# A fused transformer block on one core: two-head chunks in place of four-head ones in the attention products, paired 64-row remainders in the first dense layer, DMA transposes, and a shared PSUM bank

## The chip, the cores and the metric

The kernel runs on one core of a Trainium2 chip. The metric is the device time of one execution in microseconds (us), as the median of several runs. The profile is one further execution, in which the hardware profiler records each instruction. Its span, from first to last instruction, is some 2 us shorter than the device time.

Engines: PE is TensorE (matrix products), PEld is its weight load, DVE is VectorE, ACT is ScalarE, POOL is GpSimd, SP issues most DMA transfers. PSUM is the memory that PE's products are summed in; here it is used as eight banks.

## The reference, cut to what matters

S = 2048 tokens, D = 448, H = 16 heads of 28 features, F = 1792.

```python
xn  = layernorm(x)                                   # no scale, no bias
q, k, v = split(xn @ wqkv)                           # 16 heads of 28
phi_q = concat(softmax(q@w_phi), softmax(-q@w_phi))  # 56 features a head
phi_k = concat(softmax(k@w_phi), softmax(-k@w_phi))
kv  = phi_k^T @ v ;  z = sum over tokens of phi_k    # one 56 x 28 matrix a head
o   = (phi_q @ kv) / (phi_q @ z + 1e-6)
out = x + o @ wo + silu(xn @ w1) @ w2
```

This is linear attention: kv needs all tokens, so no token's output can start before the last token's key is done. The two dense layers (dense 1 is `xn @ w1`, dense 2 is `silu(..) @ w2`) depend on nothing of attention, and can fill gaps. `w_phi` is multiplied into the q and k weights on the chip at the start (the "fold").

## The kernel before: the parts that matter

The program is built from operations with reads, writes, a priority and a guessed duration. A list scheduler on the host orders them once. On the chip every engine then works through its own fixed list, and waits on semaphores where an operand comes from another engine. Priority 0 is the most urgent.

```python
# dense 1: contraction 448 = 4 x 112 rows; one silu per block
for kt in range(4):
    e.matmul(hps, w1_sb[:, kt, ft*128:(ft+1)*128], xnT_sb[:, kt, tok0:tok0+ntok], ...)   # 112 rows
act(hT[:, ft, ...], hps, Silu)

# keys: token-major, all + signs (s=0), then all - signs (s=1); chunks of four heads
for s in range(2):
    for g in range(4):
        e.matmul(bank[3+s][0:112, g*116:(g+1)*116], Ek[:, sl, s, g*112:(g+1)*112],   # 112 columns of weights
                 vaug[:, sl, 4*g:4*g+4, :])                                          # 4 x 29 = 116 columns

# queries: feature-major (EqT), not normalised; U has 4 heads x 30 = 120 columns
for s in range(2):
    for g in range(4):
        e.matmul(bank[3+s][:, g*120:(g+1)*120], EqT[:, cs, g, s, tokens], KVZ[:, s, g])
# DVE: R2, Dd, den, rden, Gq, then o12 (896 elements in f32); POOL: o_sum = o12[+] + o12[-]
# PE: 4 transposes of o_sum; ACT: copy; PE: wo

# dense 2 of a tile: own bank, ACT copies it to Y_sb, POOL adds x; after wo, DVE adds Y_sb
```

Here `vaug` is v with a column of ones for each head, so that one product gives kv and z. A block of four heads against four heads makes a 112 x 116 product of which only the four blocks on the diagonal are wanted; a mask removes the others.

The softmax here doesn't subtract the row's maximum and nothing guards it: scores larger than these inputs give would overflow.

## Time and profile before

187.69 us median (187.44 to 188.22, 4 runs). From the page of the profile: first busy time and share per engine, then the granted TensorE clock in 40 slices of the span (in tenths), then the chain of work that ended last.

```profile
span 185.7 us, 3256 instructions
...
PE 176.4 (95%) x1272; PEld 105.1 (57%) x1272; DVE 96.0 (52%) x215; ACT 99.9 (54%) x197; POOL 75.6 (41%) x94
...
PEclk9999999999999999999999999999999999999997
...
PE 77%; DVE 7%; DMA 6%; SPq 4%; POOL 2%; issue 1%; ACT 1%; POOLq 0%; DVEq 0%; ACTq 0%
...
```

PE is busy for 95% and makes up 77% of the chain. The clock is at full speed up to the last slice (0.7), which lies after the last product. But the busy time of PE is not its work: the products overlap, and the mean of one in the groups (352 ns for 448 columns) is a latency. The work is what one product adds to a stream of them. The chain of waits, which merges neighbours, shows it; its columns are start, duration and what.

```profile
...
58.73 12.09 PE psum L552 x56
...
108.61 1.51 PE psum L640 x8
...
```

56 products of 512 columns in 12.09 us are 216 ns each, 8 of 448 in 1.51 us are 189 ns each. The groups of instructions by line and shape give the counts: after the bar, busy us and the mean ns of one.

```profile
...
L682 POOL TENSOR_TENSOR scr<-scr 128x448 bf16<-128x448 f32 x16 | 18.1, 1134 | 33.7 <-DVE scr L676 25.3 <-PE psum L696 8.4
...
L676 DVE TENSOR_TENSOR scr<-psum,Gq 128x896 f32<-128x896 f32 x16 | 17.4, 1090 | 0.7
...
L660 PE MATMUL psum<-KVZ,EqT 112*128 112x120 bf16 x128 | 10.4, 216 | 0.0
...
L604 PE MATMUL psum<-vaug,Ek 128*112 128x116 bf16 x128 | 9.3, 214 | 0.0
...
L669 DVE SCALAR_TENSOR_TENSOR den<-Dd 128x16 f32<-128x16 f32 x16 | 6.2, 391 | 0.5
...
```

Here the reader sees the 128 key products of 116 columns (L604), the 128 query products of 120 columns (L660), the o product on DVE (1090 ns) and the addition on POOL (1134 ns). In the middle of attention, these form the chain of waits, from the query product (L660) to the transposes (L688):

```profile
...
142.75 0.43 PE psum L660 x8
...
143.82 0.37 DVE den L669
...
144.81 1.10 DVE scr L676
...
145.98 1.14 POOL scr L682
...
147.17 0.43 PE psum L688 x4
...
```

Counts times spacing, over all products but the warm-up ones, is **164.5 us of PE work**. The span splits as follows (worked out from the start of every product in the trace):

| | before, us |
|---|---|
| PE work | 164.5 |
| PE time lost up to 18.5 us, where dense 1 first runs without gaps | 10.6 |
| PE time lost from there to the last product | 7.6 |
| after the last product | 3.0 |
| span | 185.7 |

### The profile page before, as it was taken

How to read it: one execution, taken by the hardware profiler on the slowest of the kernel's cores; microseconds unless marked ns; L12 is line 12 of the kernel's file. 1: busy time of each engine (PE TensorE's matmuls, PEld its weight loads, DVE VectorE, ACT ScalarE, POOL GpSimd, SP SyncE). 2: the span in 40 equal slices, each digit the busy share in tenths (PEclk: the TensorE clock that was granted, in tenths of full speed). 3: DMA queues.
4: the chain of work that ended last, by engine and by line, in shares of the span. 5: the costliest groups of instructions: out<-in, count | busy, mean ns of one | idle time of the engine just before them, and what ended most of it. 6: DMA issues, size and time to landing. Idle time of an engine off the chain costs nothing.

```text
span 185.7 us, 3256 instructions
## 1 busy us (share of the span) xinstructions
PE 176.4 (95%) x1272; PEld 105.1 (57%) x1272; DVE 96.0 (52%) x215; ACT 99.9 (54%) x197; POOL 75.6 (41%) x94
## 2 busy tenths in 40 slices
PE   6978999999998999999999999999999999999982
PEld 6766866654444445556666666555555555555540
DVE  2439893050003000166777742478987888646762
ACT  2575496736663675838767765535444553513221
POOL 4136175000000000289888983165255235443651
PEclk9999999999999999999999999999999999999997
DMA  4999990000000000000000000001001000000011
GB/s 136 235 281 220 252 306 17 2 4 0 0 0 0 0 4 0 0 0 4 2 0 0 4 0 0 0 4 48 28 25 47 32 25 28 25 25 25 6 47 49
DMA packets 11375, 8.72 MB, mean 47 GB/s; under 512 B 992, under 2 KB 11360, under 8 KB 11360
## 3 DMA queue, kind: packets, MB, share of 16 engines
q1 hardware_dynamic: 11360, 8.51, 18.3%
q8 instruction: 10, 0.16, 0.4%
q14 instruction: 5, 0.04, 0.1%
HBM read 6.68 MB, written 1.84 MB: 46 GB/s over the span
## 4 chain that ended last, share of the span: by engine, by line
PE 77%; DVE 7%; DMA 6%; SPq 4%; POOL 2%; issue 1%; ACT 1%; POOLq 0%; DVEq 0%; ACTq 0%
PE psum L552 22%; PE psum L640 20%; PE psum L577 7%; PE psum L582 7%; DMA scr<-in_A_wqkv_dram 6%; PE psum L627 5%; PE psum L696 5%; SPq L445 4%; PE psum L604 4%; PE psum L660 3%; POOL scr L682 2%; DVE scr L676 2%; PE psum L688 2%; DVE den L669 1%; PE psum L513 1%
## 5 line engine op out<-in xcount | busy, mean ns | idle before, releaser
L552 PE MATMUL psum<-xnT_sb,w_sb 112*128 112x512 bf16 (+1 forms) x280 | 51.9, 337 | 0.8 <-ACT hT L555 0.5
L640 PE MATMUL psum<-w_sb,hT 128*128 128x448 bf16 x224 | 50.2, 352 | 0.8 <-DVE xnT_sb L541 0.6
L555 ACT ACTIVATE hT<-psum 128x256 bf16<-128x256 f32 (+1 forms) x70 | 34.4, 511 | 21.5 <-PE psum L552 21.0
L552 PEld LDWEIGHTS psum<-xnT_sb,w_sb 112*128 112x128 bf16 x280 | 26.4, 98 | 21.8 <-ACT hT L555 1.1
L645 POOL TENSOR_TENSOR Y_sb<-Y_sb,x_sb 128x448 f32<-128x448 f32 x16 | 16.5, 1033 | 52.9 <-ACT Y_sb L643 49.8
L592 DVE TENSOR_REDUCE Sk<-Ek 128x32 f32<-128x896 bf16 x16 | 17.3, 1084 | 28.4 <-ACT Ek L586 28.4
L682 POOL TENSOR_TENSOR scr<-scr 128x448 bf16<-128x448 f32 x16 | 18.1, 1134 | 33.7 <-DVE scr L676 25.3
L640 PEld LDWEIGHTS psum<-w_sb,hT 128*128 128x128 bf16 x224 | 21.0, 97 | 18.6 <-DVE xnT_sb L541 0.8
L596 POOL TENSOR_TENSOR Ek<-Ek,Rk 128x896 bf16<-128x896 bf16 x16 | 27.1, 1699 | 2.9 <-DVE Rk L594 1.7
L631 ACT ACTIVATE EqT<-psum 112x512 bf16<-112x512 f32 x32 | 17.6, 597 | 10.3 <-PE psum L627 10.3
L586 ACT ACTIVATE Ek<-psum 128x448 bf16<-128x448 f32 x32 | 15.6, 544 | 9.1 <-PE psum L577 5.0
L690 ACT ACTIVATE scr<-psum 112x512 bf16<-112x512 bf16 x16 | 9.5, 596 | 18.7 <-PE psum L688 18.7
L627 PE MATMUL psum<-xnT_sb,Wfull 112*112 112x512 bf16 x64 | 19.4, 379 | 0.0
L676 DVE TENSOR_TENSOR scr<-psum,Gq 128x896 f32<-128x896 f32 x16 | 17.4, 1090 | 0.7
L541 DVE COPY xnT_sb<-psum 112x512 bf16<-112x512 bf16 x12 | 4.8, 417 | 24.3 <-PE psum L535 24.3
L577 PE MATMUL psum<-Wfull,xnT_sb 112*128 112x448 bf16 x64 | 16.5, 352 | 0.0
L696 PE MATMUL psum<-wo_sb,scr 112*128 112x448 bf16 x64 | 14.8, 352 | 1.6 <-ACT scr L690 1.6
L643 ACT ACTIVATE Y_sb<-psum 128x448 f32<-128x448 f32 x16 | 8.8, 550 | 12.4 <-PE psum L640 5.8
L582 PE MATMUL psum<-Wfull,xnT_sb 112*128 112x448 bf16 x64 | 14.9, 352 | 0.0
L699 DVE TENSOR_TENSOR scr<-psum,Y_sb 128x448 bf16<-128x448 f32 x16 | 9.9, 620 | 6.9 <-POOL Y_sb L645 2.3
L521 DVE BATCH_NORM_STATS2 st<-x_sb 128x6 f32<-128x448 bf16 x16 | 9.6, 605 | 6.9 <-DMA x_sb<-in_A_x_dram 6.9
L665 DVE RECIPROCAL R<-psum 128x32 f32<-128x32 f32 x16 | 5.7, 357 | 11.7 <-PE psum L660 11.7
(48 smaller groups left out, 179.1 us busy)
## 6 DMA issues: line engine op xcount, KB each, us to landing
out_dram<-scr SPq DMA_DIRECT2D x16, 112.0 KB, 1.7
w_sb<-in_B_w_dram SPq DMA_DIRECT2D x7, 224.0 KB, 5.7
w_sb<-in_B_w_dram SPq DMA_DIRECT2D x1, 1568.0 KB, 14.9
x_sb<-in_A_x_dram SPq DMA_DIRECT2D x3, 448.0 KB, 8.1
scr<-in_A_wqkv_dram SPq DMA_DIRECT2D x1, 784.0 KB, 10.3
Wfull<-in_A_wqkv_dram SPq DMA_DIRECT2D x1, 392.0 KB, 10.3
wo_sb<-in_A_wo_dram SPq DMA_DIRECT2D x1, 392.0 KB, 11.0
x_sb<-in_A_x_dram SPq DMA_DIRECT2D x2, 112.0 KB, 2.4
```

The source lines that it names most:

```text
L552: P.op("pe", d_mm(ntok), lambda e, lhsT=lhsT, rhs=rhs, hps=hps, kt=kt: e.matmul(hps, lhsT, rhs, start=(kt == 0), stop=(kt == KT - 1)), rea ...
L555: P.op("act", d_act(ntok), lambda e, dsth=dsth, hps=hps: e.activation(dsth, hps, ACTF.Silu), reads=[hps], writes=[dsth], table="silu", nam ...
L577: P.op("pe", d_mm(D), lambda e, lhsT=lhsT, rhs=rhs, pkb=pkb, kt=kt: e.matmul(pkb, lhsT, rhs, start=(kt == 0), stop=(kt == KT - 1)), reads= ...
L582: P.op("pe", d_mm(D), lambda e, lhsT=lhsT, rhs=rhs, vb=vb, kt=kt: e.matmul(vb, lhsT, rhs, start=(kt == 0), stop=(kt == KT - 1)), reads=[lh ...
L592: P.op("dve", d_dve(896), lambda e, E3=E3, sl=sl: e.tensor_reduce(Sk[:, sl, :], E3, AXL.X, ALU.add), reads=[E3], writes=[Sk[:, sl, :]], na ...
L596: P.op("pool", d_pool(896, 1.77), lambda e, E3=E3, sl=sl: e.tensor_tensor(E3, E3, Rk[:, sl, :, None].broadcast_to([128, 32, DH]), ALU.mult ...
L627: P.op("pe", d_mm(512), lambda e, lhsT=lhsT, rhs=rhs, pqb=pqb, kt=kt: e.matmul(pqb, lhsT, rhs, start=(kt == 0), stop=(kt == KT - 1)), read ...
L631: P.op("act", d_act(512), lambda e, dstE=dstE, pqb=pqb, s=s: e.activation(dstE, pqb, ACTF.Exp, scale=(1.0 if s == 0 else -1.0)), reads=[pq ...
L640: P.op("pe", d_mm(D), lambda e, lhsT=lhsT, rhs=rhs, ft=ft: e.matmul(fb, lhsT, rhs, start=(ft == 0), stop=(ft == FT - 1)), reads=[lhsT, rhs ...
L676: P.op("dve", d_dve(896), lambda e: e.tensor_tensor(dsto, U4[:, :, :, 0:DH], Gq[:, q, :].rearrange("p (s h) -> p s h", s=2)[:, :, :, None] ...
L682: P.op("pool", d_pool(448, 2.26), lambda e: e.tensor_tensor(o_sum[:, q, :], o_both[:, q, 0, :], o_both[:, q, 1, :], ALU.add), reads=[o_bot ...
L696: P.op("pe", d_mm(D), lambda e, lhsT=lhsT, rhs=rhs, g=g: e.matmul(ob, lhsT, rhs, start=(g == 0), stop=(g == G - 1)), reads=[lhsT, rhs], wr ...
```

## The change

The intent is less PE work, and a shorter path through DVE and POOL in attention.

- Dense 1 contracts 3 x 128 rows and a remainder of 64. Two blocks' remainders lie in rows 0 to 63 and rows 64 to 127 of the array, and are issued one after the other, so that they may run side by side. They are batched, two or three pairs (4 or 6 products) at a time, and one pair alone once: 11 batches.
- q is computed token-major like k, normalised by POOL, and transposed by DMA (16 transposes). Half of the tiles of xn are transposed by DMA too.
- The 56 features of a head now lie together, (+28, -28), so a 112-wide chunk is two heads, and the key and query products stream 2 x 29 = 58 columns. As many products as before, half as wide.
- With normalised q, attention needs den, rden and o on DVE, and nothing on POOL.
- Half of the dense-2 tiles accumulate into the bank of wo: no eviction, no addition between. The other eight ("y tiles") are kept apart in f32, at the lowest priority, as filler for PE.
- Dense 1 begins with blocks of 512 tokens in place of 256, and one silu takes two banks (28 of 1024 columns in place of 70 smaller ones).

```diff
+ w1_sb = phT[:, 0:3, 0:FF] ; w1r_sb = phT[:, 3, 0:HF]     # rows 0-63: blocks 0-6; rows 64-127: blocks 7-13
+ def rem(st):
+     return [(banks[b0 + i], w1r_sb[64*i:64*i+64, fp*128:(fp+1)*128],
+              xnT_sb[64*i:64*i+64, 3, tok], st, not st) for i in range(2)]
+ def ffn1_group(blocks):                                   # 2 or 3 pairs
+     ops3[0][0](True)                                      # 2 x 3 full products of the first pair
+     pe_mms(rems, "ffn1_rem", ...)                         # the remainders of all pairs
+     ... fulls of the other pairs ...
...
- for kt in range(KT):  # pq_mm, 112 features x 512 tokens
+ for i in (1, 0):      # k, q: 128 tokens x 448 features, exp into E_sb as (head, sign, feature)
...
+ def kv(t):
+     for c in range(CC):                                   # 8 chunks of two heads
+         mm(banks[5][0:KP, c*2*DA:(c+1)*2*DA], E_sb[:, sl, 1, c*KP:(c+1)*KP],
+            vaug[:, t % NV, 2*c:2*c+2, :], ...)            # 58 columns, weights 112 wide
+ def phi_q(t):
+     P.op("pool", ..., phq = Eq * Rq)
+     P.dma(lambda e: e.dma_start_transpose(out=phT[:, :, t*128:(t+1)*128], in_=phq...))
...
+ den = U3[:, :, DH] + EPS_DEN ; rden = 1/den ; o = U3[:, :, 0:DH] * rden     # all on DVE
...
+ P.cur_prio = 3
+ for t in range(NYT):                # NYT = 8
+     y_tile(t, [6, 7][t % 2])        # dense 2 in a bank of its own, DVE adds x into Y_sb
+ for i, t in enumerate(order_t):     # 8, 0, 9, 1, ...
+     b = OUT_BANKS[ob_cnt[0] % 4]    # OUT_BANKS = [6, 7, 4, 5]
+     q = att(t)                      # priority 0
+     if t < NYT: finish_tile(t, q, b, Y_sb[:, t, :], True)
+     else:
+         P.cur_prio = 2 ; ffn2(t, b, False)
+         P.cur_prio = 0 ; finish_tile(t, q, b, x_sb[:, t, :], False)   # wo into the same bank
```

## The prediction

> **What bounds it now.** TensorE. The page gives PE 95% busy, the chain of waits 77% PE, and the granted clock is 0.995. Busy time counts overlapped latency, so I count start-to-start spacing from the timeline instead: 216 ns for 512 columns (56 matmuls in 12.09 us), 189 ns for 448 (14 in 2.65), 109 ns for 256, about 52 ns for the 116- and 120-column products and for transposes 56 ns. Summed over the instruction counts of the groups view (without the 64 warm-up products) this is 164.5 us of needed PE work: dense 1 48.5, dense 2 42.4, k and v 24.2, q 13.8, wo 12.1, kv and attention products 13.3, transposes and weight fold 10.2. The rest of the 185.7 us span: about 9.5 us lost before 18.5 us (weights arriving, 256-token blocks), about 2 in 18.5 to 110 us, 2 in 110 to 163, 3 in 163 to 183, and 2.8 after the last matmul.
>
> **What the change does to PE work (estimates from those spacings).**
> - Dense 1: contraction 448 = 3x128 + 64 instead of 4x112; two 64-row remainders run side by side in the array. 168x216 + 28 pairs x 216 = 42.3 us, plus about 0.2 us per switch group, 11 groups: 44.6 against 48.5. Saves 4. (The Trainium skill, "TensorEngine Tiling", Key Properties: tiles work in parallel; changing the mode drains the array. No run here shows either yet.)
> - q token-major: 64x189 instead of 64x216: saves 1.7.
> - kv and attention products in two-head chunks: 58 columns instead of 116 and 120, same count. If streaming alone counted, about 27 ns each and 6.5 us saved; the 112-column weight load of the kv product may hold it near 50. I take 3.3.
> - 8 of 16 xn tiles transposed by DMA: 32 PE transposes less, 1.8.
> Sum: 154 us, so about 10.3 saved.
>
> **Other engines.** The DVE/POOL chain in attention (2.5 us, then a POOL add of 1134 ns) becomes den, rden, o, about 1.1 us, without a POOL step; Y evictions on ACT and POOL adds vanish. That removes most of the loss after 110 us. In the qkv phase the costs per tile are PE 2.7 us, ACT 2.7 (4x544 + 550), DVE 2.5 to 3, POOL 3.4 (two 1699 ns multiplies). POOL is slowest there, 54 us in all, but eight dense-2 tiles (21 us of PE) fill that phase to 64 us, so PE should still bind.
>
> **Start.** Wqk now comes before w1, so dense 1 starts near 10 us instead of 8; but fold and transposes run meanwhile and 512-token blocks follow. I expect 7 to 8 us lost against 9.5. Middle and end: about 6.5 us lost, and 2.8 after.
>
> **Prediction.** 154 + 7.5 + 6.5 + 2.8 = 171 us span, 1.9 more as timed: **173.0 us**, range **168.0 to 179.0**. Chances: faster by over 2% 0.93, within 2% 0.05, slower 0.02.
>
> **What would show it right.** PE still near 95% busy and first in the chain; dense-1 PE time down by about 4 us with rem pairs starting together; 58-column spacing under 52 ns; attention without DVE/POOL waits in the chain.
>
> **What would make it wrong.** Remainder pairs that don't overlap (+6 us); 58-column products held at 50 ns by weight loads (+3); POOL or ACT becoming the pace of the qkv phase (up to +8); DMA transposes taking several us each or waiting behind loads, starving attention; a start waiting for w1 past 12 us.

## The result, and the profile after

172.17 us median (171.73 to 172.53, 4 runs) against 187.69. The ratio is 0.9165, 95% interval 0.9139 to 0.919. A ratio here is the mean time of one kernel's fast runs over that of the other's in the same rounds, so it is not quite the ratio of the medians. Executions over 1.5% slower than the fastest of the same kernel are left out of the means. The same parts of the page:

```profile
span 170.6 us, 2962 instructions
...
PE 160.1 (94%) x1170; PEld 88.6 (52%) x1176; DVE 92.0 (54%) x179; ACT 85.3 (50%) x135; POOL 68.9 (40%) x82
...
PE   6779986999999999999999999999999996999993
...
PEclk9999999999999999999999999999999999999999
...
PE 81%; DVE 6%; DMA 5%; SPq 3%; POOL 2%; issue 1%; ACT 0%; DVEq 0%
...
```

PE is as busy as before, in a shorter span. Besides the start and the end, one slice is not full: the 6 near 142 us. The groups that answer to those of before:

```profile
...
L671 DVE TENSOR_TENSOR o_sb<-psum,rden 128x448 bf16<-128x448 f32 x16 | 9.7, 619 | 0.7 <-PE psum L433 0.3
...
L421 PE MATMUL psum<-vaug,E_sb 128*112 128x58 bf16 x128 | 8.8, 210 | 0.0
L421 PE MATMUL psum<-xnT_sb,phT 64*128 64x512 bf16 x56 | 8.0, 380 | 0.0
L421 PE MATMUL psum<-KVm,phT 112*128 112x58 bf16 x128 | 6.3, 190 | 0.0
...
L666 DVE TENSOR_SCALAR den<-psum 128x16 f32<-128x16 f32 x16 | 2.6, 166 | 1.8 <-PE psum L421 1.6
...
```

Both 58-column products occur 128 times, as before. Their latencies differ (210 and 190 ns), and so do their spacings: 8 key products take 28 ns for the first and 52 for each of the others (0.39 us in all), 8 query products take 0.23 us, 29 ns each. The o product is 619 ns, not 1090, and den is 166, not 391. (Six records of full dense-1 products are missing, 162 for 168. They are counted as work.) The account of the span:

| | before | after | difference | predicted difference |
|---|---|---|---|---|
| PE work | 164.5 | 153.9 | -10.6 | -10.3 |
| lost at the start (to 18.5; to 27.7 us) | 10.6 | 12.0 | +1.4 | -2.0 (9.5 to 7.5) |
| lost from there to the last product | 7.6 | 1.6 | -6.0 | -0.5 (7 to 6.5) |
| after the last product | 3.0 | 3.1 | 0 | 0 |
| span | 185.7 | 170.6 | -15.1 | -14.7 (185.7 to 171) |

(The predicted column does not add up to its last row: the prediction's account of the kernel before was 1.9 us short of the span, above all at the start, where it has 9.5 for 10.6.) The start is cut at different times, where dense 1 first runs on. At one cut, 27.7 us, the loss is 11.6 before and 12.0 after, and the rest 6.6 and 1.6. At 18.5 us, the cut of the prediction, the changed kernel has lost 9.3. And of the 5.5 us lost after 110 us before, 1.9 are left (such sums of spacings are good to some 0.3 us). So the total was right, and PE work was right, but the lost time lay elsewhere than was said. Where does PE lose time now? In the timeline of PE at the start (columns: start, duration, engine, line, operation, count, and idle time before it with the releaser):

```profile
...
12.38 3.18 PE L421 MATMUL psum<-xnT_sb,phT 128*128 128x512 bf16 x15 [0.82 <-DVE xnT_sb L440]
...
24.42 0.40 PE L433 MATMUL psum<-ident,xn_sb 128*128 128x128 bf16 x4 [0.40 <-DVE xnT_sb L440]
...
25.86 0.40 PE L433 MATMUL psum<-ident,xn_sb 128*128 128x128 bf16 x4 [0.34 <-DVE xnT_sb L440]
26.78 0.40 PE L433 MATMUL psum<-ident,xn_sb 128*128 128x128 bf16 x4 [0.52 <-DVE xnT_sb L440]
27.69 1.47 PE L421 MATMUL psum<-xnT_sb,phT 128*128 128x512 bf16 x6 [0.52 <-DVE xnT_sb L440]
...
```

Dense 1 starts at 12.38. At 24 us dense 1 of the first 512 tokens is done. Of the next four tiles' transposes, those of one tile have been fitted in before; three tiles are left, one after the other through one PSUM bank, each waiting for DVE to empty it, with some products of the fold between. Dense 1 goes on at 27.69. And in attention:

```profile
...
143.14 0.93 PE L421 MATMUL psum<-wo_sb,oT_sb 112*128 112x448 bf16 x4 [0.72 <-DVE Y_sb L651]
144.76 1.50 PE L421 MATMUL psum<-wo_sb,oT_sb 112*128 112x448 bf16 x7 [0.69 <-ACT oT_sb L436]
```

PE idles for 1.4 us (0.72 + 0.69), first for DVE writing `Y_sb`: the last y tile. The second wait is for ACT's copy of the transposed o.

### The profile page after: what moved, and what is told of

The parts are those of the page before. It is cut to its first block, busy times and chain, and to the rows that moved or that the text cites. A ratio compares the mean times of both kernels' runs of the same rounds, so it can differ in the third digit from the quotient of the medians.

```text
span 170.6 us, 2962 instructions
## 1 busy us (share of the span) xinstructions
PE 160.1 (94%) x1170; PEld 88.6 (52%) x1176; DVE 92.0 (54%) x179; ACT 85.3 (50%) x135; POOL 68.9 (40%) x82
## 4 chain that ended last, share of the span: by engine, by line
PE 81%; DVE 6%; DMA 5%; SPq 3%; POOL 2%; issue 1%; ACT 0%; DVEq 0%
PE psum L421 79%; DMA x_sb<-in_A_x_dram 5%; SPq L477 3%; PE psum L433 2%; DVE st L529 2%; POOL rstd L533 2%; DVE xn_sb L536 1%; DVE xnT_sb L440 1%; DVE mv L530 1%; DVE xn_sb L538 1%; POOL ve L531 1%; DVE Y_sb L651 0%; DVE out_sb L684 0%; ACT oT_sb L436 0%; DVEq L793 0%
## 5 line engine op out<-in xcount | busy, mean ns | idle before, releaser
L603 DVE TENSOR_REDUCE Ssum<-E_sb 128x64 f32<-128x1792 bf16 x16 | 31.8, 1985 | 42.8 <-ACT E_sb L436 42.8
L421 PE MATMUL psum<-xnT_sb,phT 128*128 128x512 bf16 (+1 forms) x218 | 44.8, 380 | 2.0 <-DVE xnT_sb L440 1.3
L611 POOL TENSOR_TENSOR E_sb<-E_sb,Rrec 128x896 bf16<-128x896 bf16 x16 | 27.1, 1699 | 41.3 <-DVE Rrec L605 41.3
L436 ACT ACTIVATE hT<-psum 128x1024 bf16<-128x1024 f32 x28 | 28.7, 1024 | 18.1 <-PE psum L421 18.1
L436 ACT ACTIVATE E_sb<-psum 128x448 bf16<-128x448 f32 (+1 forms) x68 | 33.5, 594 | 5.2 <-PE psum L433 3.9
L421 PEld LDWEIGHTS psum<-xnT_sb,phT 128*128 128x128 bf16 (+1 forms) x224 | 17.2, 97 | 27.3 <-issue 6.2
L421 PE MATMUL psum<-Wfull,xnT_sb 128*128 128x448 bf16 x128 | 29.1, 352 | 0.0
L627 POOL TENSOR_TENSOR phq<-E_sb,Rrec 128x896 bf16<-128x896 bf16 x16 | 27.0, 1700 | 0.0
L421 PEld LDWEIGHTS psum<-Wfull,xnT_sb 128*128 128x128 bf16 x128 | 12.3, 99 | 10.6
L421 PE MATMUL psum<-wo_sb,oT_sb 112*128 112x448 bf16 x64 | 14.4, 352 | 1.4 <-DVE Y_sb L651 0.7
L421 PE MATMUL psum<-wv_sb,xnT_sb 128*128 128x448 bf16 x64 | 15.2, 352 | 0.0
L436 ACT ACTIVATE vaug<-psum 128x448 bf16<-128x448 f32 x16 | 9.0, 562 | 11.6 <-PE psum L421 11.5
```

Source lines behind the costliest of these rows:

```text
L421: r = e.matmul(dst, lhsT, rhs, start=st, stop=sp, skip_group_check=True)
L436: P.op("act", d_act(n), lambda e: e.activation(dst, src, func, scale=scale), reads=[src], writes=[dst], table=table, name=name, **keys)
L603: P.op("dve", 1950, lambda e: e.tensor_reduce(Ssum[:, sl, :], E64, AXL.X, ALU.add), reads=[E64], writes=[Ssum[:, sl, :]], name="Ssum")
L611: P.op("pool", 1700, lambda e: e.tensor_tensor(E3, E3, Rrec[:, sl, 32:64, None].broadcast_to([128, 32, DH]), ALU.mult), reads=[E3, Rrec[:, ...
L627: P.op("pool", 1700, lambda e: e.tensor_tensor(dst, Eq, Rq[:, :, :, None].broadcast_to([128, CC, 4, DH]), ALU.mult), reads=[Eq, Rrec[:, sl ...
```

## The experiments

All runs below gave right results. "At 172.2" is the changed kernel. Times are medians, and where kernels of different batches are compared, the ratios to the kernel before are used too (the changed kernel: 0.9165).

**Theory.** The gain is PE work taken away, plus PE waits in attention that went with the long DVE and POOL chain. **Rivals.** The row pairs do not overlap; the narrow products gain nothing; PE has slack, so less work would not show; the waits went because of the filler and not because of the chain.

### Dense 1: the pair, the batch, and the switch

**1. No row pairs.** The remainder's weights are padded with 64 zero rows:

```diff
- for kt in range(3): ...fulls...    # and the remainders in pairs
+ for kt in range(4):                # w1r_sb rows 64 to 127 are zero
+     w = w1_sb[:, kt, ...] if kt < 3 else w1r_sb[:, ...]
+     mm(banks[b0 + i], w, xnT_sb[:, kt, tok], kt == 0, kt == 3)
```

> The changed kernel, with the 64-row remainders of dense 1 undone: the remainder of w1 is padded with 64 zero rows, so every block is four ordinary 128-row passes, 224 products of 512 columns in all and no row pairs. Theory (the pairs run side by side, and a batch costs one switch of about 0.21 us): PE work +28x0.216 = +6.0 us, less 11 switches of 0.21 us = -2.3, so 172.2 + 3.7 = about 175.9 us. Rival (the pairs run one after the other and their gain is nil): about 170, faster by the switches.

Measured: 176.42 us (176.36 to 176.82), ratio 0.9388. The span grew by 3.8 us, where 3.7 was expected.

**2. 64 rows, but both of a pair in rows 0 to 63.**

```diff
- w1r_sb[64*i:64*i+64, fp*128:...], xnT_sb[64*i:64*i+64, 3, tok]
+ w1r_sb[0:64, (fp + i*FP)*128:...], xnT_sb[0:64, 3, tok]
```

> The changed kernel, batches and 64-row products kept, but both remainders of a block lie in rows 0 to 63, so that no two can run side by side. Theory: the start-to-start spacing of a pair's second product rises from some 4 ns to 216 ns, +28x0.216 = +6.0 us, about 178.2 us; if the switch itself is paid for a change of the rows in use, it stays. Rival (no overlap in the changed kernel): unchanged at 172.

Measured: 178.62 us (178.28 to 180.83), ratio 0.9526; the span is 6.5 us longer. In the trace, the second product of a pair starts 216 ns after the first here, and 3 ns after it in the changed kernel. The pairs do overlap.

**3. One batch per pair**, 28 in place of 11:

```diff
- ffn1_group([b + ([1, 3, 5][i],) for i, b in enumerate(blocks[pos:pos + 3])])
+ ffn1_group([blocks[pos] + ([1, 3, 5][pos % 3],)])
```

> The changed kernel, with the remainders done block by block (28 batches) in place of 11 batches. Theory (each batch costs about 0.21 us of drained array): +17x0.21 = +3.6 us, about 175.8 us. Rival (a batch costs nothing): 172.

Measured: 176.73 us (175.28 to 178.18), ratio 0.9374. One of the four executions was slow; the median of the other three is 175.88, or +3.7 us. The profiled one is the fastest, with a span of +2.8. In the trace the last full product before a batch takes 312 ns to the next start in place of 216, and the last pair of a batch 318: about 0.2 us per batch, half on the way in and half on the way out. Run 2 has the same 0.2 us with all products in the same rows, so it is paid for the 64-row shape, and not for the pairing. The Trainium skill, "TensorEngine Tiling", Key Properties, says that changing the tiling mode drains the engine; this trace agrees, and puts the two numbers above to it.

### The two products of 58 columns

**4. Weights of the key product 128 wide.** Sixteen columns of the next chunk are loaded as well; their output rows are not read.

```diff
- mm(banks[5][0:KP, c*2*DA:(c+1)*2*DA], E_sb[:, sl, 1, c*KP:(c+1)*KP], ...
+ mm(banks[5][:, c*2*DA:(c+1)*2*DA], E_sb[:, sl, 2*D + c*KP:2*D + c*KP + 128], ...   # E_sb padded by 16
```

> The changed kernel, with the stationary operand of the kv product 128 columns wide in place of 112 (16 columns of the neighbouring chunk, whose output rows nobody reads; result right). Theory (the kv product's 49 ns at 58 columns is its weight load: 112-column loads show 130 ns in the trace and 128-column loads 97): spacing falls to the 28 ns of the attention product, -128x0.021 = -2.6 us of PE work, about 169.6 us if PE binds the phase. Rival (49 ns comes from accumulation into one bank): spacing stays near 49 ns and the time at 172. Second rival (POOL paces the phase, 54 us of it without a pause): spacing falls, time stays.

Measured: 170.11 us (169.67 to 170.59, 6 runs), ratio 0.9056; span 168.8. From the groups by shape, the key product and its weight load in this run:

```profile
...
L422 PE MATMUL psum<-vaug,E_sb 128*128 128x58 bf16 x128 | 6.3, 190 | 0.0
...
L422 PEld LDWEIGHTS psum<-vaug,E_sb 128*128 128x128 bf16 x128 | 5.9, 98 | 2.9 <-POOL E_sb L612 0.3
...
```

The mean latency fell from 210 to 190 ns, and the median start-to-start spacing from 52 to 29 ns. So the load of 112 columns was the bound, and the accumulation was not. The Trainium skill, "TensorE: Matmul & The Clock Gate", Weight-path perf modes, says that the fast weight load is on when the number of weights is 128; the trace agrees: 98 ns for the load of 128 columns, 132 for 112. PE binds this phase too, for the time went down with the work.

**5. Query products of 106 columns**, 48 of which the next product overwrites:

```diff
- mm(ub[:, c*58:(c+1)*58], phT[0:KP, c, tk], KVm[:, c], ...)
+ mm(ub[:, c*58:c*58+106], phT[0:KP, c, tk], KVm[columns c*58 to c*58+106], ...)
```

> The changed kernel, with each of the 128 attention products streaming 106 columns in place of 58 (48 more that the next product overwrites; result right). Theory (this product is bound by its columns, 28 ns at 58, and PE binds the attention phase): spacing about 47 ns, +128x0.019 = +2.4 us, about 174.6 us. Rival (attention is paced by DVE or by waits and PE has slack there): under +0.7 us.

Measured: 174.93 us (174.48 to 176.52), ratio 0.9332; span +2.0 us. The spacing was 46 ns. This product is bound by its columns, and PE binds attention.

### The transposes of xn

**6. All 16 tiles on TensorE** (`XN_DMA0 = 16`).

> The changed kernel with all 16 tiles of xn transposed by TensorE (32 transposes and 8 copies by DVE more, no DMA transpose of xn). Theory (a PE transpose costs its 56 ns of PE and nothing else): +1.8 us, about 174. Rival (the DMA transposes, 2.5 us each, cost PE waits of their own, so taking them away gains what the transposes cost): within 0.7 us of 172.

Measured: 174.30 us (174.17 to 174.42), ratio 0.927; span +1.9. A PE transpose is worth its 56 ns. The DMA transposes landed 2.5 us (xn) and 3.1 us (q) after their issue, and PE did not wait for them.

### The long chain, and a bank that was held

**7. The attention chain made long again**, with the same PE work:

```diff
+ rhalf = 0.5 * rden                                        # DVE
- o_sb = U3 * rden                                          # DVE, 619 ns
+ o_sb = U3 * rhalf ; o2_sb = U3 * rhalf                    # DVE, 2 x 618 ns
+ o_sb = o_sb + o2_sb                                       # POOL, 1031 ns
```

> The changed kernel, with the attention chain made long again as before: o computed in two halves on DVE (619 ns and a small operation more a tile) and added on POOL (about 1 us more). PE work is the same. Theory A (the long chain is what cost the kernel before its 4 to 5 us of PE gaps after 110 us): +3 to +5 us, 175 to 177. Theory B (dense-2 tiles in between hide the chain; the gaps before came from how these were rationed): under +1.5 us.

Measured: 183.86 us (183.49 to 183.89), ratio 0.978. This is +11.7 us, and neither theory had said so. First, PE stands in one place:

```profile
...
142.63 0.39 PE L423 MATMUL psum<-KVm,phT 112*128 112x58 bf16 x8 [0.47 <-DVE o_sb L676]
144.94 0.40 PE L423 MATMUL psum<-KVm,phT 112*128 112x58 bf16 x8 [1.92 <-DVE o_sb L676]
...
150.84 0.57 PE L423 MATMUL psum<-KVm,phT 112*128 112x58 bf16 x8 [3.00 <-DVE o_sb L676]
151.37 1.68 PE L423 MATMUL psum<-wo_sb,oT_sb 112*128 112x448 bf16 x4
153.73 3.17 PE L423 MATMUL psum<-wo_sb,oT_sb 112*128 112x448 bf16 x8 [0.69 <-ACT oT_sb L438]
...
```

From 142.6 to 151.3 us PE runs query products, a tile's eight every 2.3 to 3.6 us, each waiting for DVE to finish an o and free a bank, and one tile's transposes. No dense-2 work lies in between. The reason shows on DVE:

```profile
...
125.53 0.61 DVE L653 TENSOR_TENSOR Y_sb<-psum,x_sb 128x448 f32<-128x448 f32 x1
...
150.70 0.61 DVE L653 TENSOR_TENSOR Y_sb<-psum,x_sb 128x448 f32<-128x448 f32 x1
...
```

The eviction of the last y tile comes at 150.70. PE's last dense-2 product before that stretch was over by 142.2, so the y tile was ready, but DVE's list, made by priority, had its eviction behind the o's of later tiles. Until it is evicted its bank (7) is not free, and `OUT_BANKS` gives that bank to the second tile of attention. Its wo products start at 151.37, just as the eviction ends (150.70 + 0.61). PE loses some 8 us from 142 us to here, where the changed kernel loses 1.8 in all.

The clock takes a further part. From the page of this run:

```profile
PEclk9999999999999999999999999999999955599999
```

From 145.5 to 159.1 us the granted clock is 0.50. The eight wo products from 153.73 on follow each other at 373 ns, where products of 448 columns take 189 in the rest of the trace; so about 3.5 us of PE time after 151.4 go to the clock (an estimate from these spacings). The mean clock of all four executions is 0.96 to 0.97. The drop comes while PE stands idle, and run 8, without the hold, does not have it before its last product; no run separates it from the hold.

The changed kernel has a like pair of events, wo at 143.14 just after this eviction on DVE:

```profile
142.46 0.62 DVE L651 TENSOR_TENSOR Y_sb<-psum,x_sb 128x448 f32<-128x448 f32 x1 [1.49 <-PE psum L421]
```

But there DVE had waited 1.49 us for PE, which finished the y tile only then: the low priority made it late on PE, and not on DVE.

**8. The long chain again, with the y tiles at priority 1 in place of 3**, ahead of attention's own dense-2 tiles (2):

```diff
- P.cur_prio = 3
+ P.cur_prio = 1
  for t in range(NYT):
      y_tile(t, [6, 7][t % 2])
```

> The run with the long attention chain (e7_chain, 183.9 us) with one thing more: the eight dense-2 tiles that are kept apart have a higher priority than the dense-2 tiles of attention, so that their PSUM banks come free before attention needs them. Theory (e7_chain lost most of its 11.7 us to a bank held by the last of these tiles, finished on PE at 142 us and evicted by DVE at 150.7, and not to the chain itself): 174 to 177 us. Rival (the chain itself costs 11 us, being DVE's pace): stays above 181.

Measured: 176.93 us (176.52 to 177.35), ratio 0.941. The hold, with the half clock that came with it, was 7 us of run 7's loss.

**9. The changed kernel with that priority alone.**

> The changed kernel with that priority alone. Theory (the changed kernel's own PE gap of 1.9 us between 142 and 146 us is the same held bank): the gap goes, -1.5 to -2 us, about 170.5. Rival (the gap is the attention chain's latency): within 0.5 us of 172.2.

Measured: 171.20 us (170.31 to 174.10, 6 runs), ratio 0.9103, interval 0.9055 to 0.9152. One execution, the 174.10, was slow; the median of the other five is 170.97. The busy times by stretch, in the changed kernel and in this run (first column the stretch, then its length and PE's busy time):

```profile
...
142.00:151.00 9.00, 7.59 (x60) 4.28 (x58) 5.71 (x12) 3.47 (x6) 0.00 (x0) 1.00 0.20 64
...
```

```profile
...
142.00:151.00 9.00, 9.00 (x88) 5.62 (x87) 6.55 (x17) 2.39 (x4) 0.00 (x0) 1.00 0.12 39
...
```

The gap is gone, and the profiled span is 2.0 us shorter (168.6). The fast medians and the ratios both put the gain at 1.2 us, and the intervals just overlap; this is the least certain of the gains. Between runs 8 and 9 only the chain differs: 0.941 against 0.9103 is 5.8 us. **That is what the rebuilt long chain costs here**, by its waits and its DVE work together. It is near the 5.5 us that the kernel before lost after 110 us, but it is not the same chain: from 142 to 167 us it keeps DVE busy for 23.8 us, where the old one took 18.1. That the short chain gave back the 3.6 us regained after 110 us is thus likely, but not shown by undoing the change itself.

**10. Fewer y tiles**, 4 in place of 8:

```diff
- NYT = 8 ; order_t: 8, 0, 9, 1, ...
+ NYT = 4 ; order_t: 4, 5, 6, 0, 7, 8, 9, 1, ...
```

> The changed kernel, with 4 in place of 8 dense-2 tiles kept apart as filler for the qkv phase; the other 12 share a bank with wo. PE work is the same, less 4 evictions on DVE. Theory (POOL needs 54 us for the phase whatever PE does, and PE stays busy only because 8 dense-2 tiles, 21 us, fill it): PE falls idle by 6 to 10 us before attention begins, 178 to 182 us. Rival (PE work alone decides, the filler's place does not matter): 172.

Measured: 173.05 us (171.88 to 173.69), ratio 0.9204 (0.7 us more than the changed kernel, within the intervals). The theory fell. It took POOL's 54 us for a wall before attention, but POOL's list interleaves two multiplications per tile, and only the keys' are needed first:

```profile
...
118.50 0.60 PE L421 MATMUL psum<-vaug,E_sb 128*112 128x58 bf16 x8
119.59 1.50 PE L421 MATMUL psum<-w_sb,hT 128*128 128x448 bf16 x7 [0.49 <-DVE Y_sb L651]
...
122.45 0.62 PE L421 MATMUL psum<-KVm,phT 112*128 112x58 bf16 x16
...
```

```profile
...
119.13 1.70 POOL L611 TENSOR_TENSOR E_sb<-E_sb,Rrec 128x896 bf16<-128x896 bf16 x1 [0.68 <-DVE Rrec L605]
120.79 5.01 POOL L627 TENSOR_TENSOR phq<-E_sb,Rrec 128x896 bf16<-128x896 bf16 x3
```

Attention's first query products (KVm) run at 122.45, while POOL still normalises queries of three later tiles until 125.8. With less filler the keys end sooner and attention starts 3.3 us sooner than in the changed kernel (125.79). By the busy times of the stretches PE idled for 1.8 us between 112 and 126 us, where the changed kernel has no gap, and won 1.4 of them back between 142 and 151, where no y tile held a bank.

### The start

**11. The tiles of tokens 512 to 1023 early.**

```diff
- P.dma(..., n / 340.0, ...)          # the scheduler's guess of the load rate, bytes per ns and partition sum
+ P.dma(..., n / 270.0, ...)
+ P.cur_prio = -1
+ for t in range(4, 8): ln_tile(t)
+ P.cur_prio = 0
```

> The changed kernel, same instructions, but the layer norm and transposes of tokens 512 to 1023 get priority over dense 1 of the first 512 tokens, and the scheduler's model of the loads is set to the measured rate. Theory (the 3.3 us that PE loses from 24 to 28 us is four tile transposes left to the end of the first chunk, one after another through one PSUM bank): that gap goes, about -2.5 us, 169.7 us. Rival (the tokens arrive too late, at 15 us, for any order to help): the wait moves to an earlier place, within 0.7 us of 172.

Measured: 170.53 us (169.77 to 170.77, 6 runs), ratio 0.9069; span 168.9.

```profile
...
19.83 0.39 PE L433 MATMUL psum<-ident,xn_sb 128*128 128x128 bf16 x4
...
21.34 0.40 PE L433 MATMUL psum<-ident,xn_sb 128*128 128x128 bf16 x4
...
26.04 1.47 PE L421 MATMUL psum<-xnT_sb,phT 128*128 128x512 bf16 x6 [0.18 <-ACT hT L436]
...
```

The four tiles' transposes now lie between dense-1 products (18.1 to 23.1 us, idle time none), and the gap of 24 to 28 us is gone. The expectation was -2.5 us; the span and the median say -1.7 and -1.6. The tokens do land early enough (15.1 us); the fixed order was to blame. (Both edits, the guess and the priority, act on that order alone; they were not tried one by one.) Before 12.4 us nothing changed.

**12. Runs 4, 9 and 11 together.**

> The 128-column kv weights, the early layer norm of tokens 512 to 1023 and the priority of the separate dense-2 tiles together. If the three gains lie on PE's path one after the other they add: 172.2 - 2.1 - 1.6 - 1.7 = about 166.8 us. If POOL's 54 us or the loads pace what is left, at least 168.5.

Measured: **166.46 us** (166.09 to 166.84, 6 runs), ratio 0.8849 (0.8813 to 0.8884). It beats both kernels: PE is busy for 96% of a span of 165.0 us. The gains add, and a little more: 2.1 + 1.2 + 1.6 us (the fast medians of runs 4, 9 and 11 against 172.2) make 4.9, and it is 5.7 us faster.

```profile
span 165.0 us, 2974 instructions
...
PE 158.8 (96%) x1176; PEld 86.0 (52%) x1176; DVE 91.8 (56%) x179; ACT 85.3 (52%) x135; POOL 68.9 (42%) x83
...
```

## Why the prediction was right, point by point

- **PE bound (right).** Every run that added or took PE work moved the time by about that work: +3.8, +6.5, +2.8 (+3.7 by the fast medians), +2.0, +1.9 us of span in runs 1, 2, 3, 5 and 6, for +3.7, +6.0, +3.6, +2.4 and +1.8 expected; -1.8 in run 4 for -2.6.
- **Dense 1, 4 us saved (right).** Run 1, which undoes it, costs 3.8 us. The pairs overlap (run 2), the switch costs 0.2 us per batch (run 3).
- **58 columns, 3.3 us saved (right).** The key product is held at 49 ns on average by its weight load, the query product runs at 29; both had been named as possible, and runs 4 and 5 show each. From 53 and 52 ns this is 128 x (4 + 23) ns = 3.5 us.
- **q token-major, 1.7 us.** No run undid it; the spacings (189 for 216 ns, 64 products) are in the trace. It was only argued.
- **xn transposes, 1.8 us (right).** Run 6: 1.9.
- **Start, 9.5 to 7.5 us lost (wrong).** The step that failed is "I expect 7 to 8 us lost against 9.5". It is 12.0. Dense 1 did not start near 10 us but at 12.4, and 2.6 us went at 24 to 28 us on the last three tiles' transposes at the end of a list, which no part of the diff names. Run 11 gets most of the latter back. What delays the 12.4 us is not settled: no run aimed at it, and in the profiles of the twelve runs dense 1 starts between 11.4 and 13.9 us.
- **Middle and end, 6.5 us lost (wrong).** It is 1.6. The prediction said that the short chain "removes most of the loss after 110 us", but then kept most of that loss in the sum. Runs 8 and 9 put a chain of about the old length at 5.8 us. The two misses cancel: 7.5 + 6.5 = 14.0 predicted, 12.0 + 1.6 = 13.6 found. That the total came out so near is luck to that extent; the part that was understood is the PE work.
- **POOL slowest in the qkv phase, hidden by eight y tiles (half right).** PE did bind. But run 10 shows that four y tiles do nearly as well, so POOL's 54 us are no wall.

What stays open: the start before 12.4 us, how much of run 9's gain is more than the spread of its fast executions (170.3 to 172.7), and whether the idle stretch brought the half clock of run 7.

## What to carry to other kernels

Count work as start-to-start spacing times number, not as busy time; where one engine binds, a change's gain can then be summed from its parts, and each part checked by undoing it. Look at what each product is bound by: a narrow product may be bound by its weight load, and a wider load (128 columns in place of 112) can be the faster one. With fixed lists per engine, filler at the lowest priority must not hold a resource that urgent work needs; the same long chain cost 11.7 us with a held bank and 5.8 without. And look at the clock of each run: part of those 11.7 us was a clock at half speed, which the waits alone do not show.

## What the Trainium skill lacked or had wrong

- "TensorEngine Tiling", Key Properties: the price of changing the mode is not given. Here a batch of 64-row products between 128-row products costs 0.10 us going in and 0.10 us coming out, for one to three pairs (the changed kernel, runs 2 and 3).
- "TensorE: Matmul & The Clock Gate", Back-to-back issue gap: it gives about 131 ns per product of 512 columns and 81 ns per one of 128 for streams with weight loads. Here such streams run at 216 ns and, for the transposes (four to eight in a row), 56 ns; the formula that the page gives for isolated products fits them. And by its LDWEIGHTS formula a load of 112 columns takes 93 ns (an estimate, 112 / 1.2), but products with such loads follow each other at 52 ns, so that formula is not the rate of a stream.
- "SBUF — State Buffer" says that VectorE and GpSimd share a port pair, and that for a VectorE instruction in a 2-port mode or with two SBUF inputs, the one that comes second is blocked for the other's whole instruction. The trace agrees; what is missing is an example of what that does to a tiny operation. In run 7, halving 16 numbers a partition on DVE takes 0.17 us alone, and mostly 0.73 us where it meets POOL's addition, with which it ends. In the kernel before, den (16 numbers) took 0.17 us in the seven tiles where POOL was idle, and 0.36 to 0.92 in eight where POOL was adding x (0.19 in one, near the end of such an addition); its mean was the 391 ns of the groups. From run 7, DVE and then POOL (145.29 + 0.73 and 144.96 + 1.03 end together):

```profile
...
145.29 0.73 DVE L672 TENSOR_SCALAR rhalf<-rden 128x16 f32<-128x16 f32 x1
...
149.42 0.17 DVE L672 TENSOR_SCALAR rhalf<-rden 128x16 f32<-128x16 f32 x1
...
```

```profile
...
144.96 1.03 POOL L678 TENSOR_TENSOR o_sb<-o_sb 128x448 bf16<-128x448 bf16 x1 [1.37 <-DVE den L668]
...
```
